# One attention-and-gate kernel: kv of batch 1 placed ahead of the first gate product, added warm products, one block-diagonal table for the last 64 frequencies, and the last copies shared out anew

## The chip, the cores and the metric

The kernel runs on one core of a Trainium2 chip. The metric is the device time of one execution in microseconds (us). Before the change the median of six runs is 230.02 us, from 229.75 to 230.12. Times inside an execution are counted from the start of its span.

## The reference: what is computed

Per batch and head (8 batches, 8 heads, 576 positions, 64 wide), attention without a softmax, a root-mean-square norm, and on the joined heads (512 wide) a gate with a long convolution:

```python
kv = np.einsum('bhsd,bhse->bhde', k, v)
o = np.einsum('bhsd,bhde->bhse', q, kv)
rms = np.sqrt(np.mean(o * o, axis=-1, keepdims=True) + 1e-06)
x = joined_heads(o / rms * g_norm)                   # [8, 576, 512]
x1, x2, x3 = split(x @ w_proj, 3)                    # each [8, 576, 512]
X2 = np.fft.rfft(x2, n=576, axis=1)
H = np.fft.rfft(filter_fft, n=576, axis=0)
y = x1 * np.fft.irfft(X2 * H, n=576, axis=1) * x3
out = y @ w_out
```

## The kernel before

The batches run one after the other, in a software pipeline: while batch b goes through the convolution, batch b+1 goes through attention. TensorE does all products and transposes, with bf16 operands. Its results go to PSUM, into tiles from a pool of four buffers (`ps_tile`); ScalarE (ACT) and VectorE (DVE) bring them from there to SBUF. GpSimd (POOL) issues the loads, in one queue, and does some additions. SyncE (SP) issues most stores, and ACT some of the last ones.

The pieces of the work are functions, each of which issues instructions in the order of the calls:

- `kv(b)` (L277) multiplies k and v of all heads: 48 small products in batch 1. Two ACT copies put the result into the block-diagonal `kvblk`. It needs k and v of the batch in SBUF; for batch 1 they come by `load_kv(1, (0, 8))` (L183), which issues k and then v behind the filter, the weights and q.
- `att_o(b, j)` (L314) multiplies `kvblk` with the transposed q of two heads. ACT squares the result (`sq`), and then DVE or ACT scales it by g_norm (`osb`). `att_r` (L329) sums the squares by a product with `ind`, and ACT makes `rstd` of it. `att_x` (L340) multiplies the two on DVE, for four heads at a time, and `fold` (L347) makes the sums and differences `ab` and `rr` from them, on DVE.
- `proj13(b, dc, parts)` (L489) is the gate product: part 0 gives x1 (8 products of 288 columns, copied by ACT), part 2 gives x3 (8 products, multiplied with x1 by DVE into `g13`). `proj2` (L410) gives x2, from the folded rows.
- `fft(b, g)` (L454) is the transform of x2 in three groups of frequencies; group 2 is the last 64. It has four products on the two halves `lo` and `hi` of the partitions: two that take all 128 rows and give 64 each, and two of 64 by 64 (L485 and L486), whose tables are `FW[lo, 1, 4]` and `FX[hi, 3]`. The tables are made by `tables` (L249) from transposes of `IV`, and copied by DVE.
- `inv` (L506) transforms back, `outp` (L552) is the output product. `last` (L591) ends the last batch: it makes the gated rows `yg` in pieces, and calls `out1` (L575) five times, each with a product, a copy by one engine (`ev`) and two stores (`qs`).
- `warm(n)` (L656) issues n products that nothing reads.

From L667 to L720 `pinned` is set, and the instructions of TensorE, ACT and DVE keep the order in which the code issues them. This is the order by hand for batches 0 and 1 (L663 to L719). After it the loop at L722 does the batches 1 to 7. The engines take their own instructions in order. A tile's PSUM buffer is given on when its last reader is done, so a product can wait for a copy of an earlier tile.

Of the kernel before, what the change touches and what calls it, by code (L numbers as in the profile page):

```python
# [20 lines left out]
def kernel(  # L21
# [16 lines left out]
    nc = tc.nc  # L38
    B, H, S, D = q.shape
    DM = H * D  # L40
# [81 lines left out]

    FX = consts.tile([P, 4, P], BF16)
    nc.vector.memset(FX[0:96, 0], 0.0)

    load_q(0)

# [119 lines left out]
    FW = consts.tile([P, 2, 6, P], BF16)  # L247

    def tables():  # L249
        d = psp.tile([P, 2, 8, P], BF16, name="ps_ft", tag="ps")  # L250
        d0, d1 = d[:, 0], d[:, 1]
        lo, hi = slice(0, 64), slice(64, P)
        tr, cp = eng.tensor.transpose, eng.vector.tensor_copy
        for i in range(2, 6):
            tr(d0[:, i], IV[:, i, 0:P], ident)
        tr(d0[0:96, 0], IV[:, 0, 0:96], ident)
        tr(d0[96:P, 6], IV[:, 1, 0:32], ident)
        for r in (lo, hi):
            tr(d0[r, 7], IV[:, 1, 32:96], ident)
        for i in range(2, 6):  # L260
            tr(d1[lo, i], IV[:, i, P:SB], ident)
        for i in (3, 5):
            tr(d1[hi, 6 + i // 5], IV[:, i, P:SB], ident)

        def copies():
            cp(out=FW[:, 0, 2:6], in_=d0[:, 2:6])
            cp(out=FW[lo, 1, 2:6], in_=d1[lo, 2:6])
            cp(out=FX[hi, 2:4], in_=d1[hi, 6:8])
            cp(out=FW[0:96, 0, 0], in_=d0[0:96, 0])
            cp(out=FX[96:P, 0], in_=d0[96:P, 6])  # L270
            cp(out=FX[:, 1], in_=d0[:, 7])
        return copies
# [4 lines left out]
    def kv(b, j0=0, j1=NDC):  # L277
        (km, vm), (kt, vt) = kvm[b % 2], kvt[b % 2]
        kvp = ps_tile("ps_kv")
        for j in range(j0, j1):  # L280
            n, nc_ = (96, 6) if b < 2 else (P, NSC)
            for c in range(nc_):
                for hp in range(2):
                    h = 2 * j + hp
                    kk, vv = (km[:n, h, c], vm[:n, h, c]) if b < 2 or c < 4 else (kt[:, h], vt[:, h])
                    mm = eng.tensor.matmul(kvp[64 * hp:64 * hp + 64, 0, j * D:(j + 1) * D], kk, vv,
                                          start=(c == 0), stop=(c == nc_ - 1))
        for h in range(2):
            r = slice(64 * h, 64 * h + 64)
            o_ = kvblk[b % 2][r, j0:j1, r]  # L290
            i_ = kvp[r, 0, j0 * D:j1 * D].rearrange("p (j e) -> p j e", e=D)
            eng.scalar.copy(out=o_, in_=i_)
# [21 lines left out]
    def att_o(b, j):  # L314
        s = st[b]
        if j == 0:
            s['sq'] = work.tile([P, NDC, S], BF16, name="sq", tag="sq")
            s['o'] = work.tile([P, NDC, S], BF16, name="osb", tag="osb")
        op = ps_tile("ps_o")
        for h in range(2):  # L320
            eng.tensor.matmul(op[:, h, 0:TH], kvblk[b % 2][:, j], s['qT'][:, 2 * (j % 2) + j // 2, h * TH:(h + 1) * TH], start=True, stop=True)
        eng.scalar.activation(out=s['sq'][:, j].rearrange("p (a b) -> p a b", a=2), in_=op[:, :, 0:TH], func=AF.Square)
        o_ = s['o'][:, j].rearrange("p (a b) -> p a b", a=2)
        if b == 0 and j < 3 or b == 1 and j != 2:
            eng.vector.tensor_scalar_mul(out=o_, in0=op[:, :, 0:TH], scalar1=g_col)
        else:
            eng.scalar.activation(out=o_, in_=op[:, :, 0:TH], func=AF.Copy, scale=g_col)
# [12 lines left out]
    def att_x(b, jp):  # L340
        s = st[b]
        if jp == 0:
            s['x'] = work.tile([P, NDC, S], BF16, name="x", tag="x", bufs=2)
        r = slice(2 * jp, 2 * jp + 2)
        eng.vector.tensor_mul(out=s['x'][:, r], in0=s['o'][:, r], in1=s['rstd'][:, r])
# [108 lines left out]
    def fft(b, g):  # L454
        x2 = st[b]['x2']
        if g == 1:
            st[b]['Y'] = work.tile([P, 6, DM], BF16, name="Y", tag="Y")
        Y = st[b]['Y']
        xp = ps_tile("ps_X")
        mm = eng.tensor.matmul  # L460
        lo, hi = slice(0, 64), slice(64, P)
        if g < 2:
            n = N1 if g == 0 else P
            if g == 0:
                mm(xp[:n, 0], FW[0:96, 0, 0, 0:n], x2[0:96, 0], start=True, stop=True)
                for c in range(2):
                    mm(xp[:n, 1], FX[:, c, 0:n], x2[:, c], start=(c == 0), stop=(c == 1))
            else:
                for ri in range(2):
                    mm(xp[:, ri], FW[:, 0, 2 + ri], x2[:, 2 + ri], start=True, stop=False)  # L470
                mm(xp[:, 0], FW[lo, 1, 2], x2[lo, 4], start=False, stop=True)
                mm(xp[:, 1], FX[hi, 2], x2[hi, 4], start=False, stop=True)
            t_ = work.tile([P, 2, 2, DM], FP32, name="tpw", tag="tpw", bufs=2)
            eng.vector.tensor_mul(out=t_[:n, 0], in0=xp[:n], in1=HH[:n, g, 1:3])
            eng.vector.tensor_mul(out=t_[:n, 1], in0=xp[:n], in1=HH[:n, g, 0:2])
            if g == 0 and b == B - 1:
                nc.gpsimd.tensor_add(out=Y[:n, 1], in0=t_[:n, 1, 0], in1=t_[:n, 1, 1])
                return lambda: eng.vector.tensor_add(out=Y[:n, 0], in0=t_[:n, 0, 0], in1=t_[:n, 0, 1])
            if g or b == 0:
                nc.gpsimd.tensor_add(out=Y[:n, 2 * g:2 * g + 2], in0=t_[:n, :, 0], in1=t_[:n, :, 1])  # L480
                return
            return lambda: eng.vector.tensor_add(out=Y[:n, 2 * g:2 * g + 2], in0=t_[:n, :, 0], in1=t_[:n, :, 1])
        for i, r in enumerate((lo, hi)):
            mm(xp[r, 0], FW[:, 0, 4 + i, r], x2[:, 2 + i], start=True, stop=False)
        mm(xp[lo, 0], FW[lo, 1, 4, lo], x2[lo, 4], start=False, stop=True)  # L485
        mm(xp[hi, 0], FX[hi, 3, hi], x2[hi, 4], start=False, stop=True)  # L486
        eng.vector.tensor_mul(out=Y[:, 4:6], in0=xp[:, 0:1].to_broadcast([P, 2, DM]), in1=HM)

    def proj13(b, dc, parts=(0, 2)):  # L489
# [85 lines left out]
    def out1(b, c0, ev, ot, qs):  # L575

        yg, blk = st[b]['yg'], c0 // 64
        pp = ps_tile("ps_out")
        for dc in range(NDC):
            kw = dict(start=(dc == 0), stop=(dc == NDC - 1))  # L580
            if blk != 6:
                eng.tensor.matmul(pp[:, 0], yg[:, dc, c0:c0 + P], wo[:, dc], **kw)
            else:
                for i, y in enumerate((yg[:, dc, c0:c0 + 64], yt[0][:, dc, 4 * P:S])):
                    eng.tensor.matmul(pp[64 * i:64 * i + 64, 0], y, wo[:, dc], **kw)
        ev(out=ot, in_=pp[:, 0])
        for i in range(2):
            qs[i].dma_start(out=o_rows(b, blk + i) if blk != 6 or i == 0 else o_rows(b - 1, NR - 1),
                            in_=ot[64 * i:64 * i + 64])

    def last(b):  # L591
# [8 lines left out]
        for h in (1, 0):  # L600
            for dc in range(NDC):
                cs, c0 = slice(dc * P, (dc + 1) * P), dc % 2 * M
                pp = tiles[h][:, dc // 2]
                for g in (1, 2):
                    eng.tensor.matmul(pp[:, c0:c0 + P], Y[:, 2 * g + h, cs], IV[:, 2 * g + h, 0:P],
                                     start=(g == 1), stop=(g == 2))
# [22 lines left out]
        for c, x, y in ((0, ua[:, :, 0:P], r(0, P)), (SB * 2 + 64, s2(64, SB), r(64, SB))):  # L629
# [16 lines left out]
        act, dve = eng.scalar.copy, eng.vector.tensor_copy  # L646
        q0, q1, q2 = nc.sync, nc.scalar, nc.gpsimd
        ot = lambda tag, bufs: work.tile([P, 4, DM] if tag == "tpw" else [P, 2, DM] if tag == "ot" else [P, 3, DM],
                                         FP32, name="ot_", tag=tag, bufs=bufs)[:, 0]
        for c0, ev, tag, bufs, qs in ((0, act, "ot", 3, (q0, q2)), (7 * 64, act, "tpw", 2, (q0, q2)),  # L650
                                      (6 * 64, dve, "ff", 1, (q0, q1)), (2 * 64, act, "ot", 3, (q0, q1)),
                                      (4 * 64, dve, "tpw", 2, (q0, q1))):
            out1(b, c0, ev, ot(tag, bufs), qs)


    def warm(n):  # L656

        pp = ps_tile("ps_w")
        for _ in range(n):
            tc.keep_in_program_order(nc.tensor.matmul(  # L660
                pp[:, 0], ind, kvblk[1].rearrange("p a b -> p (a b)"), start=True, stop=True))
# [1 line left out]
    warm(14)  # L663
    qtr(0)
    filter_angles()
    warm(9)
    pinned[0] = True  # L667
    kv(0, 0, 2)
    att_o(0, 0)
    att_o(0, 1)  # L670
    warm(2)
# [2 lines left out]
    att_x(0, 0)  # L674
    fold(0, 0)
    kv(0, 2, 4)
    warm(2)
    att_o(0, 2)
    att_o(0, 3)
    att_r(0, 2)  # L680
# [16 lines left out]
    gen_h(2)  # L697
    qtr(1, (1,))
    fft(0, 2)
    proj13(0, 0, (0,))  # L700
    kv(1)
    proj13(0, 1, (0,))
    att_o(1, 0)
    att_o(1, 1)
    proj13(0, 0, (2,))
    att_r(1, 0)
    att_r(1, 1)
    att_x(1, 0)
    att_o(1, 2)
    fold(1, 0)  # L710
    att_o(1, 3)
# [2 lines left out]
    att_r(1, 3)  # L714
    proj13(0, 2, (0,))
    att_x(1, 1)
    proj13(0, 2, (2,))
    fold(1, 1)
    proj13(0, 3)  # L719
    pinned[0] = False  # L720
    fins = [inv(0, (0, 1))]
# [81 lines left out]
```

## Time and profile before

| what | value |
|---|---|
| median of 6 runs | 230.02 us (229.75 to 230.12) |
| the profiled execution | 230.16 us, of which its span is 228.0 us |
| TensorE (PE) busy | 212.0 us, 1977 products |
| weight loads (PEld) busy | 128.3 us |
| VectorE (DVE) busy | 193.3 us, 369 instructions |
| ScalarE (ACT) busy | 158.8 us, 233 instructions |
| GpSimd (POOL) busy | 67.8 us |
| mean granted TensorE clock | 0.99 of full |
| DMA | 27.18 MB moved, mean 119 GB/s |

How to read it: the profile is of one execution, and its times are a little over the median. A row of the timeline has its start, its length, the engine, the line, the operation, what it writes and reads, the shape and the number of instructions; in brackets stand the idle time of the engine just ahead of it and what ended it. Most instructions have line 65, a helper that issues them, so they are told apart by the names of their tiles: `ps_x` stands for the gate products and for `proj2`, `ps_X` for the transform, `ps_r` for the sums of squares, `ps_w` for `warm`. `PE` is the product and `PEld` the weight load ahead of it. The chain of waits follows the last instruction back to what released it, step by step.

The stages of the execution: the start with the tables and batch 0 (0 to 36 us), batch 1's attention among the gate products of batch 0 (36 to 45 us), the loop (from then on about 24 us a batch), and the last batch's end (from about 201 us).

### The profile page before, as it was taken

The numbers are of one execution on the slowest core, as the hardware profiler recorded it, in microseconds if no ns is written. First come the engines' busy times: TensorE is split into PE (matmuls) and PEld (weight loads), VectorE is DVE, ScalarE is ACT, GpSimd is POOL, SyncE is SP. The second block draws the span as 40 slices with busy tenths as digits, with TensorE's granted clock in tenths as the row PEclk, the third lists the DMA queues.
The fourth block names the chain that finished last, engine by engine and source line by source line (L and its number), as shares of the span: only waits on it lengthen the run. The fifth ranks groups of instructions, "written<-read, shape, count | busy, mean of one in ns | idle before, by whom it ended". The sixth has DMA issues, their size and how long they took to land.

```text
span 228.0 us, 4905 instructions
## 1 busy us (share of the span) xinstructions
PE 212.0 (93%) x1977; PEld 128.3 (56%) x1977; DVE 193.3 (85%) x369; ACT 158.8 (70%) x233; POOL 67.8 (30%) x83
## 2 busy tenths in 40 slices
PE   4968899899999999999999999999999999999980
PEld 1433347575667566756665576656675666547630
DVE  6778986897997989798888989797979897999950
ACT  2739978937877697868885997769776978633340
POOL 7974009941720074005600380003000210006010
PEclk9988999999999999999999999999999999999999
DMA  6999999999994369742992299050033003500356
GB/s 63 164 222 233 199 203 141 160 190 189 184 188 104 92 81 184 141 123 37 182 204 39 60 165 215 29 134 1 5 90 92 3 0 95 132 6 3 92 128 194
DMA packets 42347, 27.18 MB, mean 119 GB/s; under 512 B 20132, under 2 KB 37540, under 8 KB 42326
## 3 DMA queue, kind: packets, MB, share of 16 engines
q0 software_dynamic: 37040, 17.70, 59.7%
q1 hardware_dynamic: 5046, 8.79, 14.7%
q10 hardware_dynamic: 240, 0.39, 0.6%
q8 instruction: 15, 0.25, 0.4%
q14 instruction: 6, 0.05, 0.1%
HBM read 33.69 MB, written 9.44 MB: 189 GB/s over the span
## 4 chain that ended last, share of the span: by engine, by line
PE 82%; ACT 8%; DVE 3%; DMA 3%; issue 1%; POOL 0%; DVEq 0%; POOLq 0%
PE ps_x L65 38%; PE ps_out L65 13%; PE ps_X L65 7%; PE ps_qT L65 4%; PE ps_r L65 3%; PE ps_o L65 3%; PE ps_kv L65 3%; DMA qb<-in_q_dram 3%; PE ps_invo L65 3%; PE ps_inve L65 3%; PE ps_h L65 2%; PE ps_w L660 2%; ACT sq L65 1%; ACT rstd L65 1%; ACT x L65 1%
## 5 line engine op out<-in xcount | busy, mean ns | idle before, releaser
L65 PE MATMUL ps_x<-x,wp 128*128 128x288 bf16 x512 | 69.2, 286 | 0.4 <-ACT rstd L65 0.2
L65 PEld LDWEIGHTS <-wp 128*128 128x128 bf16 x512 | 49.2, 98 | 14.5 <-issue 1.4
L65 ACT CAST x<-ps_x 128x576 bf16<-128x576 f32 (+2 forms) x56 | 41.1, 740 | 14.0 <-PE ps_x L65 12.7
L480 POOL TENSOR_TENSOR Y<-tpw 128x1024 bf16<-128x1024 f32 (+1 forms) x9 | 21.2, 2358 | 77.9 <-DVE tpw L65 77.9
L65 DVE TENSOR_TENSOR tpw<-ps_X,HH 128x1024 f32<-128x1024 f32 (+1 forms) x32 | 37.7, 1218 | 3.3 <-PE ps_X L65 2.7
L65 PE MATMUL ps_out<-wo,yg 128*128 128x512 bf16 (+1 forms) x160 | 34.2, 380 | 0.4 <-DVE yg L631 0.4
L65 DVE TENSOR_TENSOR g<-ps_x,x 128x576 bf16<-128x576 f32 x32 | 24.1, 752 | 10.6 <-ACT x L65 7.6
L65 ACT ACTIVATE rstd<-ps_r,bias_eps 128x576 bf16<-128x576 f32 x32 | 23.5, 746 | 5.4 <-PE ps_r L65 5.2
L65 ACT COPY ot<-ps_out 128x1024 f32<-128x1024 f32 (+1 forms) x17 | 15.9, 938 | 15.9 <-PE ps_out L65 15.9
L88 POOL DMA_DIRECT2D km<-in_k_dram x9 | 7.6, 845 | 57.9 <-PE ps_kv L65 56.2
L65 PE MATMUL ps_x<-wp,ab 128*64 128x512 bf16 (+1 forms) x128 | 23.4, 383 | 0.1
L65 PEld LDWEIGHTS <-yg 128*128 128x128 bf16 (+1 forms) x160 | 13.8, 100 | 15.8 <-issue 1.7
L65 ACT ACTIVATE sq<-ps_o 128x576 bf16<-128x576 f32 x32 | 20.5, 651 | 2.5 <-PE ps_o L65 1.8
L65 DVE TENSOR_TENSOR u<-ps_inve,os 128x576 bf16<-128x576 f32 x28 | 19.8, 748 | 2.6 <-ACT os L65 2.6
L65 ACT ACTIVATE osb<-ps_o,g_col 128x576 bf16<-128x576 f32 x26 | 19.2, 740 | 0.0
L65 PE MATMUL ps_X<-x,FW 128*128 128x512 bf16 (+4 forms) x56 | 16.4, 390 | 0.6 <-DVE tpw L65 0.5
L65 PEld LDWEIGHTS <-ab 128*64 128x64 bf16 (+1 forms) x128 | 8.4, 103 | 14.6 <-issue 5.0
L65 ACT COPY os<-ps_invo 128x576 f32<-128x576 f32 x14 | 9.0, 640 | 10.5 <-PE ps_x L65 5.1
L65 ACT COPY qT<-ps_qT 128x1152 bf16<-128x1152 bf16 x14 | 15.7, 1119 | 0.9 <-PE ps_qT L65 0.2
L65 PEld LDWEIGHTS <-Y 128*128 128x128 bf16 (+1 forms) x208 | 13.9, 97 | 2.6 <-issue 1.6
L65 PE MATMUL ps_r<-sq,ind 128*128 128x288 bf16 x64 | 13.4, 295 | 1.5 <-ACT sq L65 0.8
L65 PE MATMUL ps_o<-qT,kvblk 128*128 128x288 bf16 x64 | 12.7, 289 | 1.9 <-ACT kvblk L65 1.9
(156 smaller groups left out, 320.1 us busy)
## 6 DMA issues: line engine op xcount, KB each, us to landing
out_dram<-ot SPq DMA_DIRECT2D x28, 256.0 KB, 3.3
qb<-in_q_dram POOLq DMA_DIRECT2D x16, 288.0 KB, 6.6
km<-in_k_dram POOLq DMA_DIRECT2D x6, 512.0 KB, 6.9
vm<-in_v_dram POOLq DMA_DIRECT2D x6, 512.0 KB, 8.2
wp<-in_moe_w_proj_dram POOLq DMA_DIRECT2D x3, 512.0 KB, 10.2
out_dram<-ot SPq DMA_DIRECT2D x6, 128.0 KB, 3.7
km<-in_k_dram POOLq DMA_DIRECT2D x2, 288.0 KB
vm<-in_v_dram POOLq DMA_DIRECT2D x2, 288.0 KB
```

Of the source, the lines that this page charges most:

```text
L65: i = getattr(self.e, op)(*args, **kw)
L88: nc.gpsimd.dma_start(out=kvm[b % 2][i][:n, h0:h1, 0:C].rearrange("p h c d -> p h (c d)"), in_=bass.AP(tensor=src.tensor, offset=src.offse ...
L480: nc.gpsimd.tensor_add(out=Y[:n, 2 * g:2 * g + 2], in0=t_[:n, :, 0], in1=t_[:n, :, 1])
L660: tc.keep_in_program_order(nc.tensor.matmul(pp[:, 0], ind, kvblk[1].rearrange("p a b -> p (a b)"), start=True, stop=True))
```

## The change

Four edits. In the order by hand, `kv(1)` stands ahead of batch 0's first gate product instead of behind it, the second gate product's first part stands behind the attention of batch 1's first four heads, and `fold(1, 1)` ahead of a gate product. `warm` has 10, 3 (new, between `kv(0, 0, 2)` and `att_o(0, 0)`) and 3 products in place of 9, none and 2. The two 64 by 64 products of the last 64 frequencies become one of 128 by 128, with a table that holds both blocks and zeros elsewhere. In `last`, the third call copies by ACT instead of DVE, the fourth by DVE instead of ACT, and the fifth by ACT for one half of the columns and by DVE for the other.

```diff
     nc.vector.memset(FX[0:96, 0], 0.0)
+    nc.vector.memset(FX[:, 3], 0.0)
...
-        for i in range(2, 6):
+        for i in (2, 4):
             tr(d1[lo, i], IV[:, i, P:SB], ident)
...
-            cp(out=FW[lo, 1, 2:6], in_=d1[lo, 2:6])
-            cp(out=FX[hi, 2:4], in_=d1[hi, 6:8])
+            cp(out=FW[lo, 1, 2], in_=d1[lo, 2])
+            cp(out=FX[hi, 2], in_=d1[hi, 6])
+            cp(out=FX[hi, 3, hi], in_=d1[hi, 7, hi])
+            cp(out=FX[lo, 3, lo], in_=d1[lo, 4, lo])
...
-        mm(xp[lo, 0], FW[lo, 1, 4, lo], x2[lo, 4], start=False, stop=True)
-        mm(xp[hi, 0], FX[hi, 3, hi], x2[hi, 4], start=False, stop=True)
+        mm(xp[:, 0], FX[:, 3], x2[:, 4], start=False, stop=True)
...
-        ev(out=ot, in_=pp[:, 0])
+        for e, cs in ev:
+            e(out=ot[:, cs], in_=pp[:, 0, cs])
...
-        for c0, ev, tag, bufs, qs in ((0, act, "ot", 3, (q0, q2)), (7 * 64, act, "tpw", 2, (q0, q2)),
-                                      (6 * 64, dve, "ff", 1, (q0, q1)), (2 * 64, act, "ot", 3, (q0, q1)),
-                                      (4 * 64, dve, "tpw", 2, (q0, q1))):
+        al, ha, hb = slice(0, DM), slice(0, DM // 2), slice(DM // 2, DM)
+        for c0, ev, tag, bufs, qs in ((0, ((act, al),), "ot", 3, (q0, q2)), (7 * 64, ((act, al),), "tpw", 2, (q0, q2)),
+                                      (6 * 64, ((act, al),), "ff", 1, (q0, q1)), (2 * 64, ((dve, al),), "ot", 3, (q0, q1)),
+                                      (4 * 64, ((act, ha), (dve, hb)), "tpw", 2, (q0, q1))):
...
-    warm(9)
+    warm(10)
     pinned[0] = True
     kv(0, 0, 2)
+    warm(3)
     att_o(0, 0)
...
     kv(0, 2, 4)
-    warm(2)
+    warm(3)
     att_o(0, 2)
...
     fft(0, 2)
+    kv(1)
     proj13(0, 0, (0,))
-    kv(1)
-    proj13(0, 1, (0,))
     att_o(1, 0)
     att_o(1, 1)
     proj13(0, 0, (2,))
     att_r(1, 0)
     att_r(1, 1)
     att_x(1, 0)
+    proj13(0, 1, (0,))
     att_o(1, 2)
...
     att_x(1, 1)
+    fold(1, 1)
     proj13(0, 2, (2,))
-    fold(1, 1)
     proj13(0, 3)
```

## The prediction

> **What bounds the kernel now.** I read the page's busy shares first, then the chain of waits, the busy times by stretch, and the timeline at the three places that the change touches.
>
> ```profile
> PE 212.0 (93%) x1977; PEld 128.3 (56%) x1977; DVE 193.3 (85%) x369; ACT 158.8 (70%) x233; POOL 67.8 (30%) x83
> ...
> PE 82%; ACT 8%; DVE 3%; DMA 3%; issue 1%; POOL 0%; DVEq 0%; POOLq 0%
> ```
>
> TensorE is 93% busy and holds 82% of the chain. By stretch (the first column is the stretch, then its length and TensorE's busy time):
>
> ```profile
> 36.20:45.10 8.90, 7.74 (x99) 5.36 (x97) 6.40 (x12) 7.99 (x15) 8.89 (x10) 1.00 1.12 136
> 45.10:201.00 155.90, 155.28 (x1490) 97.75 (x1489) 138.79 (x252) 118.56 (x172) 35.84 (x35) 1.00 0.71 109
> ```
>
> From 45.10 to 201.00 TensorE has 0.6 us idle in 156: whatever it is late by at 45.10 it is late by at 201, and a product saved in that stretch is saved in full. From 36.20 to 45.10 it has 1.2 us idle, and there the order of ScalarE (ACT) and VectorE (DVE) counts:
>
> ```profile
> 36.27 1.14 PE L65 MATMUL ps_x<-x,wp 128*128 128x288 bf16 x8
> ...
> 37.34 0.95 PE L65 MATMUL ps_kv<-vm,km 96*64 96x64 bf16 x48
> ...
> 39.41 0.64 ACT L65 CAST x<-ps_x 128x576 bf16<-128x576 f32 x1 [0.34 <-PE ps_x L65]
> ...
> 39.94 1.20 ACT L65 ACTIVATE sq<-ps_o 128x576 bf16<-128x576 f32 x2
> ...
> 40.63 1.54 DVE L65 TENSOR_SCALAR osb<-ps_o,g_col 128x576 bf16<-128x576 f32 x2 [2.46 <-ACT sq L65]
> ...
> 44.28 1.39 ACT L65 ACTIVATE rstd<-ps_r,bias_eps 128x576 bf16<-128x576 f32 x2
> ```
>
> The next fence is a line of the DMA view (KB, then us from issue to landing): batch 1's v takes 15.0 us.
>
> ```profile
> vm<-in_v_dram POOLq DMA_DIRECT2D x1, 576.0 KB, 15.0
> ```
>
> The timeline has its issue at 21.70, so it lands at 36.7. The kv products start at 37.34 and never feel it. The 64-frequency transform, in the chain of waits (start, length, times):
>
> ```profile
> 56.47 0.86 PE ps_X L65 x4
> ...
> 64.46 1.73 PE ps_out L65 x8
> 66.19 0.67 PE ps_X L65 x4
> ```
>
> A 512-column product streams in 1.73/8 = 0.216 us; four full ones take 0.86. The four of the small transform take 0.67: two pairs, the members of a pair side by side, each pair 0.33 = 0.216 and 0.12 of weight load that nothing covers. Last, the tail (timeline):
>
> ```profile
> 221.51 0.59 ACT L65 COPY ot__3309<-ps_out 128x512 f32<-128x512 f32 x1 [1.85 <-PE ps_out L65]
> 221.94 0.69 DVE L65 COPY ot__3318<-ps_out 128x512 f32<-128x512 f32 x1 [1.21 <-PE ps_out L65]
> ...
> 222.70 0.93 ACTq L588 DMA_DIRECT2D out_dram<-ot__3318  x1
> 223.13 0.76 SPq L588 DMA_DIRECT2D out_dram<-ot__3318  x1
> ```
>
> **What the Trainium skill says.** "TensorE: Matmul & The Clock Gate", Part 3, section "The mechanism": a weight load runs under a product in flight only when its rows differ from the product's, or it goes to the background buffer. The trace agrees as far as it goes: full after full has no gap, and each change between full, half-column and quarter shapes costs about 0.12. The same page, Part 1 ("What's actually happening"): a free-running window of 3.4 us with too little work halves TensorE's clock. Here the granted clock is 0.50 from about 15.3 to 18.7, after TensorE sat idle from 13.0 to 14.9 before the first o product. "PSUM — Partial Sum Buffer", section "PSUM bank collisions raise a hardware error": two engines on one bank at once collide, so a scheduler puts them one after the other. No row of before shows two engines reading one tile at once; in the built order of the changed kernel the DVE half does wait for the ACT half.
>
> **Step 1, the start (warm 9 to 10, 3 new, 2 to 3; table; memset).** With products between kv and o the clock should stay up. At most that removes the 0.52 that ACT waits for ps_r at 17.06, and the extra product ahead of kv takes back 0.22: 0.3 gained. If the clock falls anyhow, five products more cost up to 0.4. The three new ones wait for a buffer that DVE's second qT copy frees at 13.37, which is ahead of the o product at 14.89. The two transposes fewer, two small DVE copies more and the memset are under 0.3 together. All this moves only when TensorE arrives at 36.27, and step 2 waits for v until 36.83, 0.56 later: I price step 1 at zero in both directions. If that cover is gone it is worth -0.3 to +0.4.
>
> **Step 2, kv(1) ahead.** kv now stands where TensorE arrives at 36.27, but v lands at 36.7; with 0.13 to the first product it starts at 36.83 and ends 0.88 later (37.34 to 38.22 in before), 37.71. Behind this wait on TensorE's queue stands all that follows: the first gate product, o, the norms. The gate product that hid this landing comes behind it, 0.98, to 38.69. ACT's cast of it begins 0.21 after (39.20 to 39.41 in before), 38.90; sq 0.53 behind, 39.43, which is 0.51 earlier than before; osb on DVE 40.12. The first ps_r ends at 40.40, rstd 40.61. The second ps_r waits for osb's buffer (40.12+0.81+0.07 = 41.00), second rstd 41.45.
> So far it is half a microsecond ahead. But the second gate product, whose cast ACT did at 39.41 in before, now comes here. TensorE gives it the PSUM buffer of the first rstd (ended 41.36), so it runs 41.42 to 42.40, with the third and fourth o behind it. ACT has nothing from 42.09 (second rstd's slot of 0.64) to the cast at 42.61. Then sq 43.14, osb 43.67, sq 44.29, rstd 44.82, each at before's spacing (0.53, 0.62, 0.53); before has that rstd at 44.28. Its end, 0.75+0.07 later, frees the buffer for the products at 45.10: now 45.64. DVE's fold(1,1) ahead of a gate multiply (0.67) makes rr ready at about 49.2, but those products end at 50.4, so it buys nothing. Step 2: +0.53, to be carried to the end. Bounds: DMA landing 0.2 either way, so +0.3 to +0.75.
>
> **Step 3, block-diagonal table.** Per transform one pair goes (0.33) and one full product comes (0.216); the load before it is still bare (0.12), the one behind it is hidden: 0.67 becomes 0.216+0.12+0.216 = 0.55, 0.12 saved. Batch 0's lies ahead of v's landing and is worth nothing; batches 1 to 7 give 7 x 0.12 = 0.84. In batch 7 it passes on by the ACT copies of ps_out and osa, which wait for TensorE. A full-size load behind a pair shows in no row of this place: it could be hidden too (0.24 saved each), or the load behind could stay bare (0 saved): -1.68 to 0, value -0.84.
>
> **Step 4, tail.** The third last copy goes from DVE to ACT and is 0.1 shorter (0.59 for 0.69), but its DMA on SP's queue stands behind one that issues until 220.80, and SP is then busy until 221.99 in either kernel: zero. The copy of the last block but one moves to DVE: products done at 220.99, so 221.03 to 221.72, 0.37 earlier than ACT's 222.09 (ACT was issuing DMAs until 221.33). But ACT's DMA of that block now waits for DVE, issues until 222.30, and ACT's half copy stands behind it: 222.34 to 222.71 (the 128x256 copy osb took 0.37). DVE's half waits for ACT's: 222.77 to 223.19 (0.41, the 128x256 ub row). Both last DMAs go at 223.22; in before SP's went at 223.13 and ACT's at 222.70. SP's is 0.1 later. +0.1, bounds -0.15 (two together landed in 3.4 to 3.6 in before, the last one in 3.8) to +0.35.
>
> **Sum.** 0 + 0.53 - 0.84 + 0.1 = -0.2 us. The profiled execution was 230.16 (span 228.0, 2.16 around it), so 229.96 there; the median of the runs is 0.14 below it: 229.8.
>
> **Rivals.** (a) V is not the gate: if it lands 0.5 earlier than its row says, kv starts at 36.27 or sooner, step 2 is +0.53-0.56, about 0, and step 1's 0.3 comes through: -0.84-0.3+0.1 = -1.0, 229.0. For it: only one landing is seen. Against: the 16 engines are busy all the way to it, and nothing in the change alters the loads. (b) The slower end: ACT's hole behind rstd (0.53, at 42.1 to 42.6) is not paid back because the full-size load in the transform stays bare on both sides. Then +0.53+0.1, and up to 0.2 from a slow tail: 230.7. It decides once a transform saves less than 0.09 (0.63/7), and can be measured under 0.03. Against it: full after full shows no gap in any row. (c) The split does nothing: it is in step 4 already, as the halves run one after the other.
>
> **How the numbers follow.** A measurement of this kernel tells about 0.2% (0.46 us) from no change. Forecast 0.66, own range 229.4 to 230.3 (0.13 of it below 229.56, 0.53 within); (a) 0.21, faster; (b) 0.13, of which 0.12 slower. Faster 0.34, same 0.54, slower 0.12. Range 228.9 to 230.5, which leaves 0.09 of (a) and 0.1 of (b) out.
>
> **What would show it.** Step 1: clock 1.00 from 15 to 19, earlier sq at about 19. Step 2: TensorE idle until about 36.8 ahead of ps_kv, the dense stretch beginning at 45.6. Step 3: ps_X x3 in 0.55 in the chain. Step 4: half copies one after the other at 222.3 and 222.8 (less the shift). A kv start at 36.3 or a dense stretch before 45.1 makes step 2 wrong; ps_X x3 in 0.65 makes step 3 wrong.

## The result, and the profile after

The changed kernel takes 229.68 us (median of 34 runs, 228.63 to 231.75), the kernel before 229.93 beside it (71 runs). The ratio is 0.9992 with a 95% interval from 0.9983 to 1.0001: no difference that this measurement can tell. The prediction was 229.8. The profiled execution took 229.59 with a span of 227.7, against 230.16 and 228.0 before. Here and below a median is over all executions, while a ratio leaves out the few in a second, slower state that an execution of any of these kernels can fall into (one in run 2, three in run 7, two in run 8 and two of before beside runs 5 to 8).

The page: the busy shares, and under part 4 the chain of waits by engine.

```profile
PE 210.9 (93%) x1972; PEld 127.9 (56%) x1972; DVE 193.5 (85%) x372; ACT 158.7 (70%) x234; POOL 67.7 (30%) x83
...
PE 76%; DMA 13%; POOL 3%; ACT 3%; DVE 1%; issue 1%; ACTq 0%; POOLq 0%; DVEq 0%
```

TensorE is as busy as before, but DMA has gone from 3% of the chain to 13%: the load of v has come onto the path (6%), and ahead of its issue that of the filter (5%). The busy times by stretch (stretch, length, TensorE's busy time; the granted clock is the first of the last three columns) show where. Here is a piece of the start, before and then after, and the two stretches that the prediction used, after:

```profile
15.00:18.70 3.70, 3.70 (x36) 1.91 (x35) 3.29 (x5) 2.82 (x6) 1.14 (x3) 0.54 1.15 261
```

```profile
15.00:18.70 3.70, 3.42 (x41) 1.74 (x39) 3.06 (x5) 3.00 (x7) 0.78 (x1) 1.00 1.14 271
...
36.20:45.10 8.90, 7.30 (x96) 5.49 (x97) 6.34 (x14) 6.90 (x13) 8.88 (x10) 1.00 1.31 158
45.10:201.00 155.90, 154.94 (x1486) 97.78 (x1485) 138.67 (x250) 118.57 (x174) 34.19 (x33) 1.00 0.70 107
```

The clock stays at 1.00 from 15.0 to 18.7, where the kernel before has 0.54. In the middle TensorE does 0.44 us less than before in the same window (7.30 for 7.74), and in the long stretch it is idle for 1.0 us of 156 (0.6 before), so it is still the bound there. The first product of the last small transform before (timeline):

```profile
35.46 0.74 PE L65 MATMUL ps_X<-x,FW 128*64 128x512 bf16 x3
```

The timeline of the middle after, with rows of TensorE and of ACT:

```profile
34.71 0.41 PE L65 MATMUL ps_X<-x,FW 128*64 128x512 bf16 x2
...
36.64 0.95 PE L65 MATMUL ps_kv<-vm,km 96*64 96x64 bf16 x48 [1.20 <-DMA vm<-in_v_dram]
...
42.40 0.64 ACT L65 CAST x<-ps_x 128x576 bf16<-128x576 f32 x1 [0.39 <-PE ps_x L65]
...
45.45 4.08 PE L65 MATMUL ps_x<-x,wp 128*128 128x288 bf16 x32 [0.23 <-ACT rstd L65]
```

The last small transform starts at 34.71, 0.75 sooner than before. What TensorE does next stands behind ACT's filling of `HM`, from 34.44 to 35.46 here and from 35.19 to 36.21 before, where the first gate product starts at 36.27. So kv could start at about 35.5 (in run 10, with v there in time, `HM` ends at 34.51 and kv starts at 34.56); it starts at 36.64, as v lands at 36.5, and that wait costs about 1.1 (the 1.20 in the row counts from the end of the last product). ACT's hole behind the rstd is there too (0.39 at 42.40), and the dense stretch, the gate products from which on TensorE hardly idles, begins at 45.45, 0.35 later than before. The small transform of batch 1, and what follows it, in the timeline, before and then after:

```profile
66.12 0.74 PE L65 MATMUL ps_X<-x,FW 128*64 128x512 bf16 x3
...
66.79 0.42 PE L65 MATMUL ps_o<-qT,kvblk 128*128 128x288 bf16 x2
```

```profile
66.47 0.41 PE L65 MATMUL ps_X<-x,FW 128*64 128x512 bf16 x2
66.81 0.39 PE L65 MATMUL ps_X<-x,FX 128*128 128x512 bf16 x1
67.03 0.41 PE L65 MATMUL ps_o<-qT,kvblk 128*128 128x288 bf16 x2
```

From its first product to the next o it takes 0.56; before it took 0.67. By the first of the five output products the lag has turned into a lead (216.71 for 217.09). The tail (timeline):

```profile
221.36 0.99 ACTq L591 DMA_DIRECT2D out_dram<-ot__3308  x1
...
222.39 0.37 ACT L65 COPY ot__3317<-ps_out 128x256 f32<-128x256 f32 x1 [2.13 <-PE ps_out L65]
222.87 0.42 DVE L65 COPY ot__3317<-ps_out 128x256 f32<-128x256 f32 x1 [1.53 <-ACT ot__3317 L65]
223.32 0.48 SPq L591 DMA_DIRECT2D out_dram<-ot__3317  x1
```

ACT's half copy stands behind ACT's store, and DVE's half behind ACT's. The last stores, ACT's with SP's, go 6.6 us after the first output product, before 6.0; yet the span ends 10.99 after it, before 10.91.

So the sum of the profiled execution is +0.35 (dense stretch), -0.73 (from there to the first output product: 171.26 for 171.99) and +0.08 (tail): -0.3, which is 227.7 for 228.0.

### The profile page after: what moved, and what is told of

The parts are those of the page before. It is cut to its first block, busy times and chain, and to the rows that moved or that the text cites. A ratio compares the mean times of both kernels' runs of the same rounds, so it can differ in the third digit from the quotient of the medians.

```text
span 227.7 us, 4902 instructions
## 1 busy us (share of the span) xinstructions
PE 210.9 (93%) x1972; PEld 127.9 (56%) x1972; DVE 193.5 (85%) x372; ACT 158.7 (70%) x234; POOL 67.7 (30%) x83
## 4 chain that ended last, share of the span: by engine, by line
PE 76%; DMA 13%; POOL 3%; ACT 3%; DVE 1%; issue 1%; ACTq 0%; POOLq 0%; DVEq 0%
PE ps_x L65 40%; PE ps_out L65 12%; PE ps_X L65 7%; DMA vm<-in_v_dram 6%; DMA fa<-in_moe_filter_fft_dram 5%; PE ps_invo L65 3%; PE ps_r L65 3%; PE ps_qT L65 3%; PE ps_inve L65 3%; PE ps_o L65 3%; PE ps_kv L65 2%; DMA out_dram<-ot 1%; ACT x L65 1%; POOL km L88 1%; ACT sq L65 1%
## 5 line engine op out<-in xcount | busy, mean ns | idle before, releaser
L483 POOL TENSOR_TENSOR Y<-tpw 128x1024 bf16<-128x1024 f32 (+1 forms) x9 | 21.2, 2359 | 75.8 <-DVE tpw L65 75.8
L65 DVE TENSOR_TENSOR g<-ps_x,x 128x576 bf16<-128x576 f32 x32 | 24.1, 752 | 10.4 <-ACT x L65 6.9
L65 PEld LDWEIGHTS <-ab 128*64 128x64 bf16 (+1 forms) x128 | 8.4, 103 | 14.6 <-issue 5.0
L65 ACT COPY qT<-ps_qT 128x1152 bf16<-128x1152 bf16 x14 | 15.7, 1119 | 0.9 <-PE ps_qT L65 0.2
L65 PE MATMUL ps_X<-x,FW 128*128 128x512 bf16 (+3 forms) x48 | 13.7, 388 | 0.6 <-DVE tpw L65 0.5
L97 POOL DMA_DIRECT2D qb<-in_q_dram x16 | 12.3, 777 | 5.8 <-DMA wp<-in_moe_w_proj_dram 3.1
## 6 DMA issues: line engine op xcount, KB each, us to landing
wp<-in_moe_w_proj_dram POOLq DMA_DIRECT2D x3, 512.0 KB, 10.7
```

What stands on the lines that cost most here:

```text
L65: i = getattr(self.e, op)(*args, **kw)
L97: nc.gpsimd.dma_start(out=qb[b % 2][64 * g:64 * g + 64].rearrange("p h (m x) -> p (h m) x", m=3), in_=bass.AP(tensor=q.tensor, offset=q.of ...
```

## The experiments

The theory, formed when the profile after was known: the table gains about 0.7, the start's gain is swallowed because the new order lets TensorE wait for v, and the tail is worth nothing. The rival: the table does little, and the gain comes from the start; or the new order is dear by itself, whatever v does. The runs came in three groups of four, each on one chip with its own runs of before (medians 229.89, 229.38 and 229.63), so the ratios are what to compare.

**1. The table alone.** Kernel before, with only the diff's lines on `FX` and the transposes:

```diff
-        mm(xp[lo, 0], FW[lo, 1, 4, lo], x2[lo, 4], start=False, stop=True)
-        mm(xp[hi, 0], FX[hi, 3, hi], x2[hi, 4], start=False, stop=True)
+        mm(xp[:, 0], FX[:, 3], x2[:, 4], start=False, stop=True)
```

> The kernel before with the block-diagonal table alone. Theory (the table pays for the other parts): each small transform takes about 0.56 us where the kernel before has 0.67, seven of them count, so the time is 0.7 to 0.8 us below before's 229.93, at 229.1 to 229.2, while the dense stretch begins at 45.1 as before. Rival (the bare weight load stays on both sides, and what was gained came from the start's clock): the row of three products takes 0.65 or more and the time is 229.9.

Measured: 228.93 (22 runs), ratio 0.9958 [0.9941, 0.9975], that is -1.0 (-1.4 to -0.6). In its profile the clock is low for longer than in before's (0.70 from 18.7 to 25.0, where before has 1.00), so the dense stretch begins at 45.80, 0.7 later; the first output product starts at 217.09 as in before. 171.29 for 171.99: 0.70 saved over seven batches. The timeline of one transform:

```profile
66.82 0.41 PE L65 MATMUL ps_X<-x,FW 128*64 128x512 bf16 x2
...
67.39 0.41 PE L65 MATMUL ps_o<-qT,kvblk 128*128 128x288 bf16 x2
```

It is 0.57 from the pair to o, the theory's number. The rival, by which the table does nothing, falls; the 0.3 by which the median gained more than the profile explains is within the interval.

**2. The order alone.**

```diff
     fft(0, 2)
+    kv(1)
     proj13(0, 0, (0,))
-    kv(1)
-    proj13(0, 1, (0,))
...
     att_x(1, 0)
+    proj13(0, 1, (0,))
...
+    fold(1, 1)
     proj13(0, 2, (2,))
-    fold(1, 1)
```

> The kernel before with the new order by hand alone (kv of batch 1 first, second gate product later, fold earlier). Theory: TensorE reaches kv at 36.3 and waits for v until 36.6 to 36.8; the second gate product behind the first rstd leaves ACT idle; the dense stretch begins at 45.45 to 45.65 instead of 45.10, and the time is 0.35 to 0.55 above before's, 230.3 to 230.5. Rival (the order costs nothing by itself, or gains because kv and the norms come sooner): 229.5 to 229.9, dense stretch at 45.1 or sooner.

Measured: 230.37 (22 runs), ratio 1.003 [1.0015, 1.0045]: +0.7 (0.3 to 1.0), the theory's sign and a little more than its size. The timeline:

```profile
37.09 0.95 PE L65 MATMUL ps_kv<-vm,km 96*64 96x64 bf16 x48 [0.72 <-DMA vm<-in_v_dram]
...
45.90 4.08 PE L65 MATMUL ps_x<-x,wp 128*128 128x288 bf16 x32 [0.23 <-ACT rstd L65]
```

V was issued at 21.24 and took 15.7, so it landed at 36.9. From kv to the dense stretch it is 8.81, as in the changed kernel. The clock falls in this start as in before's.

**3. The warm counts alone.**

```diff
-    warm(9)
+    warm(10)
     kv(0, 0, 2)
+    warm(3)
...
-    warm(2)
+    warm(3)
```

> The kernel before with the three counts of warm products changed alone. Theory: the clock does not fall to 0.50 at 15 us, the end of the first stage comes 0.75 to 1.0 us sooner, at about 35.3; the first gate product, 1.1 long, still lies ahead of kv, so kv waits for v by no more than 0.3 (from 36.4 to 36.65), and 0.5 to 0.7 of the gain reaches the dense stretch (44.5) and the end: 229.2 to 229.4. Rival (the gain of the start is swallowed by v in any order, or by ACT and DVE in the middle): dense stretch at 45.0 to 45.1, time 229.9.

Measured: 229.80 (14 runs), ratio 0.9989 [0.9969, 1.0008]. The profile agrees with the theory (the first gate product starts at 35.68, kv at 36.75 without a wait, the dense stretch at 44.51), but the median does not show 0.5 to 0.7; the interval, -0.7 to +0.2, does not shut it out either. One reason may lie in the runs of before themselves: their mean granted clock goes from 0.982 to 0.997, and those at 0.9935 or above have a median of 229.45 (16 runs), those from 0.9865 to 0.9935 of 229.95 (24), the rest of 230.39 (11). A fall to 0.50 for 3.4 us takes 0.0075 from the mean of a span of 228, so the fall that I saw in one profile is missing in these 16 at the least, and there is nothing to gain in those. The mean doesn't tell more: the profile of run 3 itself has 0.992 with no fall in the start, but one at the very end. A second reason is the landing of v, next.

**4. The changed kernel in the order of before.**

```diff
     fft(0, 2)
-    kv(1)
     proj13(0, 0, (0,))
+    kv(1)
+    proj13(0, 1, (0,))
...
     att_x(1, 0)
-    proj13(0, 1, (0,))
...
-    fold(1, 1)
     proj13(0, 2, (2,))
+    fold(1, 1)
```

> The changed kernel with the order by hand of before put back (warm counts, table and tail as changed). Theory: the sum of the start's 0.5 to 0.7, the table's 0.75 and a tail worth 0.1 or less: 228.6 to 228.8, which is 0.9 to 1.1 below the changed kernel's 229.68, with the dense stretch at 44.5. Rival (the order is not what eats the start's gain): within 0.2 of the changed kernel, dense stretch at 45.1 to 45.4.

Measured: 228.53 (only 7 runs), ratio 0.9942 [0.9919, 0.9965], the theory's number. But its profile is of its slowest execution (229.88), and shows what I had not thought of (timeline):

```profile
35.53 1.14 PE L65 MATMUL ps_x<-x,wp 128*128 128x288 bf16 x8 [0.39 <-ACT HM L65]
...
38.00 0.95 PE L65 MATMUL ps_kv<-vm,km 96*64 96x64 bf16 x48 [1.33 <-DMA vm<-in_v_dram]
...
45.76 4.08 PE L65 MATMUL ps_x<-x,wp 128*128 128x288 bf16 x32 [0.23 <-ACT rstd L65]
```

Here v was issued at 22.28, took 15.6 and landed at 37.9, more than a microsecond later than in the profiles of before and after. Even behind the gate product kv waits 1.33. (The 0.39 in brackets is too long: the record of the last small product is missing in this trace and in those of runs 1 and 5 to 8, where only its weight load is left. What ended the wait is `HM`, as in the kernel before.) The expected dense stretch at 44.5 was missed for that reason.

**5. V earlier, changed order.** The changed kernel, with this edit:

```diff
     load_wp(0)
-    load_wp(2)
     load_q(1)
     load_kv(1, (0, 8))
+    load_wp(2)
     load_w(wo, moe_w_out)
```

> The changed kernel, with q, k and v of batch 1 loaded ahead of the weights of the third part instead of behind them. Theory (v's landing at 36.5 is what swallows the start's gain in the changed order): v lands well before TensorE is done with the last small transform at 35.3, kv follows without a wait, the dense stretch begins at 44.1 to 44.4 instead of 45.45, and the time is 1.0 to 1.3 below the changed kernel's 229.68: 228.4 to 228.7. Rival (the place of the second gate product and ACT's hole swallow it, or the weights of the third part now come late): dense stretch at 45.1 or later, 229.4 to 229.7.

Measured: 227.72 (6 runs), ratio 0.9927 [0.9899, 0.9954]: -1.7 against before, where the changed kernel has -0.2. Timeline:

```profile
34.40 0.95 PE L65 MATMUL ps_kv<-vm,km 96*64 96x64 bf16 x48 [0.39 <-ACT HM L65]
...
38.98 1.14 PE L65 MATMUL ps_x<-x,wp 128*128 128x288 bf16 x8
...
43.20 4.08 PE L65 MATMUL ps_x<-x,wp 128*128 128x288 bf16 x32 [0.23 <-ACT rstd L65]
```

V was issued at 20.61 and took 13.1: 33.7. Kv no longer waits for it, and the dense stretch begins at 43.20, 8.80 behind kv, with the second gate product in the same late place. So that place costs nothing: it is the wait for v that swallowed the gain. The changed kernel itself was measured apart from this group. Within the group run 8, below, stands for it: it has the changed kernel's loads and order, and only the tail of before. Its ratio is 1.0014, and the two intervals lie apart.

**6. V earlier, order of before.** The edits of 4 and 5 together.

> The same earlier loads, with the order by hand of before and the changed warm counts, table and tail. Theory: here the first gate product covers v's landing except where it comes late (37.9 in the profile of the run without the order, 36.5 to 37.0 in the others), so the earlier v is worth 0 to 0.4 against that run's 228.53: 228.1 to 228.5, dense stretch at 44.2 to 44.5, and the distance to the run with the changed order falls from 1.1 to 0.3 or less. Rival (the new order is dear by itself, whatever v does): the distance stays at 0.7 or more.

Measured: 227.52 (6 runs), ratio 0.9917 [0.9896, 0.9938]. The distance between the two orders is 0.2 here, where it is 1.1 with v late (0.9942 for 0.9992, from two groups). In the profile the gate product starts at 34.74 and the dense stretch at 43.58: 8.84. The theory holds: with v there, both orders are worth the same.

**7. Kv first, the second gate product where it was.** The changed kernel, with

```diff
     kv(1)
     proj13(0, 0, (0,))
+    proj13(0, 1, (0,))
...
     att_x(1, 0)
-    proj13(0, 1, (0,))
...
-    fold(1, 1)
     proj13(0, 2, (2,))
+    fold(1, 1)
```

> The changed kernel with kv of batch 1 ahead of the first gate product, but with the second gate product and the fold back at their places of before. Theory (the wait for v is the cost, the later gate product with ACT's hole neither adds nor saves much): kv at 36.6, both gate products behind it, the first o at 39.5, dense stretch at 45.3 to 45.5, time 229.5 to 229.8 as for the changed kernel. Rival (ACT's hole behind the rstd is the cost): dense stretch at 45.0 or sooner, 229.2 or less.

Measured: 229.97 (22 runs), ratio 1.0018 [0.9995, 1.0042]. Its timeline:

```profile
37.49 0.95 PE L65 MATMUL ps_kv<-vm,km 96*64 96x64 bf16 x48 [2.92 <-DMA vm<-in_v_dram]
...
46.23 4.08 PE L65 MATMUL ps_x<-x,wp 128*128 128x288 bf16 x32 [0.23 <-ACT rstd L65]
```

In this group the start is quicker (`HM` is filled at 34.9) and v late (37.4), so the wait is about 2.6; the 2.92 in the row holds the missing product. From kv to the dense stretch it is 8.74, in the changed kernel 8.81: ACT's hole is worth 0.07. The rival's 0.5 is not there.

**8. The changed kernel with the tail of before.** The lines of `out1` and `last` put back.

```diff
-        for e, cs in ev:
-            e(out=ot[:, cs], in_=pp[:, 0, cs])
+        ev(out=ot, in_=pp[:, 0])
```

> The changed kernel with the output copies of the last batch as before (one engine to a copy). Theory: the split of the last copy and the exchange of engines are worth nothing, as the halves run one after the other behind ACT's DMA: 229.5 to 229.7, within 0.15 of the changed kernel. Rival (the split brings the last stores forward): 229.9 to 230.1.

Measured: 230.43 (22 runs), ratio 1.0014 [0.9985, 1.0043]: the interval is too wide to tell the two apart. The profile tells more. Its kv waits about 3.0 for v (landing at 38.0; 3.38 in the row, with a product missing). Counted from the first output product, its last store is issued at +6.2 (changed kernel +6.6), and its span ends at +10.39. Over all the profiles with one engine to a copy and before's queues the end is at +10.4 to +10.9 (six of them), with the split copy at +10.7 to +11.05 (five). The split gains nothing and may lose 0.2.

**9. The earlier loads alone.** The edit of 5 on the kernel before.

> The kernel before with nothing changed but the loads: q, k and v of batch 1 ahead of the weights of the third part. Theory (in the order of before the first gate product covers v's landing up to about 37.3, and the profiles show landings from 36.5 to 38.0): a wait goes in some executions only, so 0 to 0.5 below the kernel before, dense stretch 8.8 us behind the start of the first gate product. Rival (v's landing is not what differs; the loads speed up the whole first stage, or cost elsewhere): more than 0.8 below, or above before.

Measured: 228.16 (6 runs), ratio 0.9939 [0.9915, 0.9962]: -1.4, far more than I expected; by its number the rival's. In the profile the gate product starts at 34.72, kv at 35.79 with no wait (v landed at 34.6), the dense stretch at 43.55. My expectation took before's start from its one profile (gate product at 36.27). Where the start is quicker, as here and in run 7, v landing at 36.5 to 38.0 holds up the order of before as well. A quicker first stage by the loads themselves is what is left of the rival, and the profiles speak against it. In the timeline of run 9 the first copy of batch 0's `kvblk`, the issue of the first load that the edit moves, and the last small transform:

```profile
13.36 0.53 ACT L65 CAST kvblk<-ps_kv 64x128 bf16<-64x128 f32 x2 [1.75 <-PE ps_kv L65]
...
14.43 0.81 POOL L97 DMA_DIRECT2D qb<-in_q_dram  x1
...
33.91 0.74 PE L65 MATMUL ps_X<-x,FW 128*64 128x512 bf16 x3
```

From the copy to the transform it is 20.55. In all eleven profiles whose clock stays up in the start it is 20.55 to 20.61, with the loads moved or not. What differs is when the copy comes (13.0 to 14.3), and in all six profiles with the loads moved it comes before the first moved load is issued (14.0 to 14.6). So the quick start isn't the work of these loads; what they gain is then the wait for v, though how long it was in the kernel before on this chip no profile shows.

**10 to 12. The tail once more**, all with the earlier loads. Run 10: the second store of the last block but one by POOL.

```diff
-(2 * 64, ((dve, al),), "ot", 3, (q0, q1)),
+(2 * 64, ((dve, al),), "ot", 3, (q0, q2)),
```

> The changed kernel with the earlier loads of batch 1, and in the tail the second store of the last block but one issued by POOL instead of ACT. The tail is counted from the first of the five output products. Theory (ACT's half copy stands behind ACT's own store, which makes it 0.8 late): the half copy begins at +4.9 instead of +5.6 to +5.7, DVE's half follows it and ends at +5.8 instead of +6.5, the last stores are issued at +5.8 to +6.2 instead of +6.5 to +6.7, and the span ends at +10.2 to +10.5 instead of +10.7 to +11.05. Rival (SP's own queue sets the last store): the half copies come sooner, but SP's last store and the end stay where they are.

Run 11: besides, the last block's halves in two PSUM banks.

```diff
+        for dc in range(NDC if blk == 4 else 0):
+            for i in range(2):
+                eng.tensor.matmul(pp[:, i, 0:DM // 2], yg[:, dc, c0:c0 + P], wo[:, dc, i * DM // 2:(i + 1) * DM // 2],
+                                  start=(dc == 0), stop=(dc == NDC - 1))
...
+            e(out=ot[:, cs], in_=pp[:, 0, cs] if blk != 4 else pp[:, i, 0:DM // 2])
```

> As the run with POOL's store, and the last output block's two column halves go to different PSUM banks (eight products of 256 columns in place of four of 512), so that ACT and DVE need not read one bank. Theory (DVE's half waits for ACT's half because both read one bank): both half copies begin within 0.15 of each other at about +4.95 and end at +5.35; the last stores are then limited by SP's earlier store, +5.5 to +6.2, and the end is that of the run with POOL's store or up to 0.4 sooner. Rival (they stand one after the other for another reason): DVE's half still begins 0.45 behind ACT's.

Run 12: the copies of before, and the first store of the last block but one by POOL.

```diff
-(2 * 64, act, "ot", 3, (q0, q1)),
+(2 * 64, act, "ot", 3, (q2, q1)),
```

> The changed kernel with the earlier loads of batch 1, the tail's copies as before (one engine to a block), and the first store of the last block but one issued by POOL instead of SP. Theory (of before's tail SP's queue is what the last store waits for): SP's last store goes right behind DVE's copy at +5.6 to +5.8 instead of +6.05 to +6.3, and the span ends at +10.1 to +10.4 instead of +10.4 to +10.9; time 0.2 to 0.5 below the run with the earlier loads. Rival (the landings set the end, whenever the store is issued): the end stays at +10.4 to +10.9.

Measured: 227.79, 227.81 and 228.14 (6, 7 and 6 runs), ratios 0.9928 [0.9903, 0.9953], 0.9923 [0.9902, 0.9945], 0.9935 [0.9912, 0.9957]: none better than run 5. Their first output products start at 214.67, 215.52 and 214.97. The timeline of run 10, with ACT's half copy and SP's last store:

```profile
219.46 0.37 ACT L65 COPY ot__3317<-ps_out 128x256 f32<-128x256 f32 x1 [1.24 <-PE ps_out L65]
...
220.93 0.55 SPq L591 DMA_DIRECT2D out_dram<-ot__3317  x1
```

The half copies in the timeline of run 11:

```profile
220.32 0.37 ACT L65 COPY ot__3317<-ps_out 128x256 f32<-128x256 f32 x1 [1.25 <-PE ps_out L65]
220.79 0.42 DVE L65 COPY ot__3317<-ps_out 128x256 f32<-128x256 f32 x1 [0.66 <-ACT ot__3317 L65]
```

And SP's last store in the timeline of run 12:

```profile
220.55 0.59 SPq L590 DMA_DIRECT2D out_dram<-ot__3317  x1
```

The first half of the theory holds: with ACT's store gone, ACT's half begins at +4.79 instead of +5.68, and everything behind it moves with it. The second half falls: SP's last store goes at +6.26 and +5.58 (runs 10 and 12) instead of +6.6, but takes 3.9 and 4.4 us to land instead of 3.0, and the spans end at +11.33, +11.38 and +11.43, later than with the split tail as it is. An earlier issue is given back in the landing. So it is without POOL among the last stores: in the eleven other profiles SP's last store is issued at +6.0 to +6.7 and lands at +9.3 to +9.8, with no gain for the earlier ones; with POOL's it lands at +10.0 to +10.2. Run 11 fails too: in two banks, DVE's half still begins 0.47 behind ACT's.

All times in one place (us from the span's start; "between" is from the start of the dense stretch to the first output product, and the last column is the span's end from the first output product):

| kernel | kv starts (wait for v) | dense stretch | first output product | between | end |
|---|---|---|---|---|---|
| before | 37.34 (0) | 45.10 | 217.09 | 171.99 | 10.91 |
| changed | 36.64 (1.20) | 45.45 | 216.71 | 171.26 | 10.99 |
| 1 table | 38.04 (0) | 45.80 | 217.09 | 171.29 | 10.71 |
| 2 order | 37.09 (0.72) | 45.90 | 217.91 | 172.01 | 10.59 |
| 3 warm | 36.75 (0) | 44.51 | 216.52 | 172.01 | 10.78 |
| 4 order of before | 38.00 (1.33) | 45.76 | 217.05 | 171.29 | 11.05 |
| 5 v early | 34.40 (0) | 43.20 | 214.48 | 171.28 | 10.72 |
| 6 v early, order of before | 35.81 (0) | 43.58 | 214.87 | 171.29 | 10.73 |
| 7 kv first | 37.49 (2.6) | 46.23 | 217.52 | 171.29 | 10.98 |
| 8 tail of before | 38.12 (3.0) | 46.92 | 218.21 | 171.29 | 10.39 |
| 9 loads only | 35.79 (0) | 43.55 | 215.54 | 171.99 | 10.76 |

The column "between" takes two values, 171.26 to 171.29 with the table and 171.99 to 172.01 without. From "kv starts" to "dense stretch" it is 8.80 to 8.81 in the changed order, 8.74 in run 7, and 7.76 to 7.77 in the order of before, whose first gate product (1.07) comes ahead of kv. Everything else is the start and the landing of v.

## Why the prediction was right, step by step

**The start (step 1), priced at zero.** Right in outcome, wrong in size. I allowed at most 0.3, from one wait of ACT. The second pair's sq came from 19.37 to 18.62 and the last small transform from 35.46 to 34.71, both 0.75 sooner. Of this 0.59 is the clock that stays up: from the first copy of `kvblk` to the transform it is 20.57 for 21.16, and run 3, whose copy comes at 14.30 as before's, has the same. The other 0.16 lies ahead of it, as the copy itself came sooner (14.14 for 14.30). The table takes nothing from batch 0 at this place, as TensorE stands behind `HM`. At half clock every product on the way is longer (four ps_r took 1.17 and take 0.95, 24 kv products took 0.85 and take 0.57), and I had counted only the wait behind the first. The cover, v, was larger than the gain, so none of it reached the end, as the step said. Its bounds for the case without cover (-0.3) were too narrow; run 3's profile has -0.59. The Trainium skill, "TensorE: Matmul & The Clock Gate", Part 1 ("What's actually happening"), says of the clock's window that it is free-running and that the effect varies from run to run. The runs of before agree: their medians go from 229.45 to 230.39 with their mean clock, and in run 9 the start of before ran without a fall. The prediction read this part of that page and still took one profile's dip for every execution's.

**Kv ahead (step 2), +0.53.** It measured +0.35 in the profile (45.45 for 45.10). Kv started at 36.64 where I had 36.83, as v landed at 36.5 and not at 36.7; the rest, 8.81 from kv to the dense stretch, is what I worked out (36.83 to 45.64, 8.81). ACT's hole appeared at the place foreseen. But it isn't a price: 8.81 against the 8.83 of before from its gate product. So the 0.53 was the wait for v alone (36.83 for 36.27), as the prediction's rival (a) reckons too. In the prediction's own sum ACT's hole only gives back what the earlier norms had gained, and run 7 puts its worth at 0.07. Rival (b) had no ground in saying that ACT's hole has to be paid back. The mechanism of rival (a) is what runs 5 and 6 show when v is made to land sooner; in the kernel as changed v was the gate.

The bound of 0.2 either way on the landing was too tight: in the eight profiles with the loads in their old place (issue and time from issue to landing added) it lies at 36.5, 36.5, 36.7, 36.7, 36.9, 37.4, 37.9 and 38.0. In the four of these with kv first it starts 0.12 to 0.15 behind the landing. In the order of before kv waits only where TensorE arrives more than 1.07, the length of the first gate product, ahead of v.

**The table (step 3), -0.84.** It measured -0.70 to -0.73: 0.10 for each of seven transforms instead of 0.12. The rows by their starts say what the step said (0.67 becomes 0.56: the pair 0.34, the full product 0.22 with nothing bare behind it). The sign I had set down for it was wrong, though. In the chain of waits of the changed kernel:

```profile
66.53 0.66 PE ps_X L65 x3
67.19 0.24 PE ps_o L65 x2
```

The row of three products has 0.66, not 0.55, and by my own words 0.65 would have made the step wrong. The chain dates a row from the end of the row before to its own end, so a bare load ahead of a product counts to that product's row. In before (66.19 0.67, then o with 0.35 at 66.86) three loads are bare: into the first pair, into the second, and out of it into o, where it makes 0.35 of 0.24. The change takes away the third, so the gain stands in the row of o (0.67 and 0.35 for 0.66 and 0.24). The sum was right since one bare load goes; I had put it in the wrong row.

**The tail (step 4), +0.1.** It measured +0.08, by two errors that cancel. ACT's store took 0.99 and not 0.54, so ACT's half came 0.4 later than I had it, measured from the first output product, and so did the last stores; and their landing took 3.0 instead of 3.8. The Trainium skill may have the reason for the first, "Perfetto Trace Analysis", section "DMA Instruction — HWDGE (DVE, Sync)": the two sequencers that issue such transfers, VectorE's and SyncE's by its wording, share one descriptor generator, and the time shown holds the wait for its lock. That ACT and SP stand in this relation here is an inference. The rows agree in part: ACT's 0.99 from 221.36 lies over an issue of SP that runs to 221.94 and the next from 222.03; but the last two, issued together at 223.32, took 0.48 and 0.50, and in before one of ACT's took 0.54 beside one of SP's (both at 222.12), which one lock doesn't explain. What makes an issue long stays open. For the second, "DMA: Bandwidth & Descriptors", section "Issuing engines are not separate DMA queues", says that the transfers run on the same 16 engines whoever issues them, and that issuing from several engines only saves the time of issue; runs 10 to 12 agree (3.9 and 4.4 us to land). As for the halves: that they run one after the other was right. The reason that the prediction gave, the shared PSUM bank, is not supported: they do so in two banks as well (run 11). Whether the tile in SBUF or the one in PSUM makes the wait was not tried.

**The sum** of -0.2 stood against -0.3 in the profiled execution and -0.25 between the medians. That it is this near owes something to errors of 0.1 to 0.2 with different signs; the two large terms, +0.35 and -0.7, were each found at their place. It was lucky also in the one landing that it had: where the start was quick and v late (the profiles of runs 7 and 8) kv ahead waited 2.6 to 3.0 in place of 1.1, and the medians lie above before's, though both intervals reach 1.

## What to carry to other kernels

A product that hides a load's landing costs the wait that it hid, up to its own length (1.07 here), when it is moved behind the load's user, and the landing must be taken as a range over executions, not as one profile's row. Before an order is changed to bring work forward, ask whether its input can be there: moving one load of 0.5 MB behind batch 1's q, k and v was worth 1.4 us in the kernel before, more than all four edits together. The fastest kernels here, runs 5, 6, 10 and 11 (ratios 0.9917 to 0.9928, not to be told apart), have the table, the warm products and that one line moved, in either order; the intervals of runs 4, 9 and 12 (0.9935 to 0.9942) overlap with theirs. Without that line moved the change pays in the order of before (run 4), and so does the table by itself (run 1).

## What the runs showed of the hardware that was not expected

- One transfer of 576 KB by POOL's queue, in the same place of the same queue, took 14.6 to 15.7 us, was issued between 21.2 and 22.8, and landed over a range of 1.5 us.
- The issue of a 128 KB store took from 0.47 (run 7) to 1.39 us (run 9) of SP's queue. The long one had an issue of ACT beside it, and so had the short one.
- A last store issued 1.0 us sooner landed no sooner (4.4 for 3.0 us), and with POOL among the last stores the span ended at +11.3 to +11.4, without it at +10.4 to +11.05. The ratios (0.9923 to 0.9935 against run 5's 0.9927) don't show that difference.
- The start of before ran with and without a fall of the clock. From the first copy of `kvblk` to the last small transform it took 21.16 (before), 21.36 (run 2) and 21.92 us (run 1) with the clock low in between, and 20.55 in run 9 with the clock at 1.00, so a fall cost 0.6 to 1.4. In before TensorE had waited 1.87 for that copy, in run 9 0.63; whether the shorter wait kept the clock up was not tried.
